# Gated attention and feed-forward on one core: scores and feed-forward in array tiles of 64 rows by 64 columns, P V in tiles of 64 by 32

## The chip, the core and the metric

The kernel runs on one core of a Trainium2 chip. The core has a matrix engine (TensorE, called PE in the profile, with its weight loads listed apart as PEld), a vector engine (VectorE, DVE), a scalar engine for activations (ScalarE, ACT), a general one (GpSimd, POOL), and a queue for transfers (SyncE, SP). The metric is the device time of one execution in microseconds (us); lower is better.

## What is computed

Two blocks read the same input `x` (2048 rows of 512) and are mixed row by row by a sigmoid gate. Block A is attention with 32 query heads of width 16 and one shared key and value head; block B is a feed-forward block with SiLU and 1792 hidden units. All arrays are float32.

```python
g = _sigmoid((x * gate_w).sum(-1, keepdims=True))
# A
q = (x @ wq).reshape(B, S, H, Dh).transpose(0, 2, 1, 3)      # H = 32, Dh = 16
k = x @ wk
v = x @ wv
p = _softmax(jnp.einsum("bhqd,bkd->bhqk", q, k) * Dh ** -0.5, axis=-1)
a = jnp.einsum("bhqk,bkd->bhqd", p, v)  # heads side by side, then @ wo
# B
b = _silu(x @ w1) @ w2
out = g * a + (1 - g) * b
```

## The kernel before

Matrix products that need float32 accuracy are made from float16 pieces: each operand is split into a float16 head and a float16 rest, and a product is the sum of three float16 products (head by head, head by rest, rest by head). A prologue transposes `x`, makes keys, values and the first queries, and splits the weights. Then `attention` runs, and nearly all of the time is spent there.

Attention goes in 32 rounds: 4 blocks of 512 query rows, 4 groups of 8 heads, and two halves of a group. A round has 16 steps, one for each 128 keys, and each step has two halves, so there are 1024 score slots in all. `scores` (L1348) makes one: two head pairs stand in the array's upper and lower 64 rows (50 of them used: the halves of q and k and the shift), and four matmuls with 32 keys each fill the 128 output rows, so 8 matmuls of 512 columns write one two-bank PSUM tile `S`. ScalarE then takes the exponent of the 128 by 1024 scores (L1369) into the float32 tile `P`. There are two `S` tiles, so the scores of half-step p wait for the exponent of half-step p-2.

`sums` (L1447) multiplies P by the values (called P V here, L1467). The stationary operand has 32 columns: the 16 value columns, a column of ones for the softmax sum, and digits. Four heads stand side by side in the 128 output rows, and the two head pairs' key halves use the upper and lower 64 rows: 8 matmuls in tiles of 64 by 32. A step is done either "native", in float32 (tile `VF`; all 512 columns in one go, or 256 and 256), or as an upper and a lower half-precision part (tiles `VP`, and `L`, which VectorE makes from P in a subtraction at L1388).

The feed-forward products, the output projection and the later query projections are a second stream of work on PE, dealt out in slots between the scores (`f_slot`, L1224). A slot holds one product of a new output block with its upper 64 rows of the contraction and one product of the block before it with its lower 64 rows: 4 + 4 matmuls of 512 columns through `Out.product` (L1007 to L1009). Where only one block is under way, the slot holds one half. ScalarE takes a tanh of each hidden block (L1023), VectorE and GpSimd finish it, and VectorE adds output blocks into accumulators (L983).

At the start of the attention loop the order of PE's work is a string written by hand, `FIRST`: S is a score slot and E one whole product of a query projection (`Out.whole`, L1013), which uses the array as one tile of 128 rows by 128 columns. After that, the order on PE, VectorE and GpSimd is fixed when the program is built, by a planner that keeps a clock for each engine: `SLOT` is its cost of a score or feed-forward slot, `VSLOT` and `NATIVE` those of P V, `issue(n, dur)` charges n instructions and dur us to PE's clock, and the `WAYS` table sets its preferences. Each engine executes its own instructions in that order and waits only on semaphores. When the last round ends, the remaining feed-forward blocks run as whole products.

Of the kernel before, what the change touches and what calls it, by code (L numbers as in the profile page):

```python
# [135 lines left out]
class Way:  # L136
# [7 lines left out]
    def set(self, p):  # L144
        for name, value in zip(self.names, WAYS[min(p // WAY_STEP, len(WAYS) - 1)]):
            setattr(self, name, value)
# [18 lines left out]
def kernel(  # L165
# [21 lines left out]
    nc = tc.nc  # L187
# [15 lines left out]
    KT = consts.tile([128, S], F16)  # L203
# [689 lines left out]
    def attention(ctx, scale_of, t_scale, shifts, split_pieces, chores, q_todo, bounds, early, gates_, later):  # L893
# [13 lines left out]
        def issue(n, dur):  # L907

            if sent[0] // 256 != (sent[0] + n) // 256:
                pe[0] = crossed[0] = max(pe[0], crossed[0] + BLOCK)  # L910
            sent[0] += n
            pe[0] += dur

        def put(dur, ready, due, f, hard=False, low=None, turns=False):

            tasks.append([due, ready, dur, f, hard, low, turns])
            return tasks[-1]
# [82 lines left out]
        class Out:  # L1000
# [5 lines left out]

            def product(self, n, rows, m, first, last):  # L1007
                l, r, i, j = self.mm[n]
                nc.tensor.matmul(self.bank[32 * m:32 * m + 32], l(i, rows, 32 * m), r(j, rows), start=first, stop=last)  # L1009

            def whole(self, n, first, last):
                l, r, i, j = self.mm[n]
# [148 lines left out]
        class Turn:  # L1161

            cur = new = None
            i = n = 0
# [47 lines left out]
        def leave(o):  # L1212

            t = o.evict(o.bank)
            f = t[3]

            def run():
                f()
                T_.free = dve[0] + 0.14

            t[3] = run
            T_.evicted = t

        def f_slot():  # L1224
            i, cur, new = T_.i, T_.cur, T_.new
            for m in range(4):
                if new and i < new.n:
                    new.product(i, lo, m, i == 0, False)
                if cur and i >= T_.n - cur.n:
                    cur.product(i - T_.n + cur.n, hi_, m, False, i == T_.n - 1)  # L1230
            issue(16, SLOT)
            if cur and i == T_.n - 1:
                leave(cur)
            T_.i += 1
            if T_.i == T_.n:
                T_.cur, T_.new, T_.going, T_.since, T_.chain = new, None, False, scored[0], bool(cur)
# [100 lines left out]
        def prefetch(i):  # L1337
            if i < len(rounds):
                c, o, rb = rounds[i]
                qtile[i] = qb_[i % 2]  # L1340
                if i:
                    assert not shifted or i == 1 or (o, c) in shifted
                    load_q(qtile[i], c, o, rb, shifts)

        probs, ends, low_end, lows, of_v, of_norm = {}, {}, {}, {}, [None], [None]
        qtile = {}

        def scores(p):  # L1348
            s, j = divmod(p, 2)
            i, kt = steps[s]  # L1350
            if p % 2 == 0 and kt == 0:
                prefetch(i + 1)
                if q_todo and i % 2 == 0:
                    queue.append(q_todo.pop(0))
            if j == 0:
                probs[s] = wp.tile([128, 4, 512], F32, name="P", bufs=PB)
            sc = pS.tile([128, 2, 512], F32, name="S")
            pe[0] = max(pe[0], ends.get(p - 2, 0.0) + 0.05)
            for m in range(4):
                for f in range(2):  # L1360
                    b = 64 * f
                    k0 = kt * 128 + 32 * m
                    nc.tensor.matmul(sc[32 * m:32 * m + 32, f], KT[b:b + 50, k0:k0 + 32], qtile[i][b:b + 50, j], start=True, stop=True)  # L1363
            issue(16, SLOT)
            begin = max(act[0], pe[0] + 0.48 - SLOT)
            scored[0] += 1
            P = probs[s]
            c, o, _ = rounds[i]
            nc.scalar.activation(P[:, 2 * j:2 * j + 2], sc, AF.Exp, scale=scale_of(c, o))  # L1369
            act[0] = begin + 0.904  # L1370
            ends[p] = begin + 1.018
            if j and s % 2 == 0:
                if s >= FIRST_LOW or not later:
                    lows[s] = put(LOW, ends[p] + 0.06, ends[p] + way.low2, lambda: low(s), low=lambda: len(L) < 2, turns=True)
                else:
                    native.add(s)
            elif j and s >= FIRST_LOW:
                lows[s] = put(LOW, ends[p] + 0.06, ends[p] + 40, lambda: low(s), low=lambda: len(L) < way.odd_l and s >= first[0] + way.spare, turns=True)
# [5 lines left out]
        def low(s):  # L1384

            P = probs[s]
            L[s] = wp.tile([128, 4, 512], F16, name="L", bufs=2)
            nc.vector.tensor_tensor(L[s], P, upper(P), op=OP.subtract)  # L1388
            low_end[s] = dve[0] + 0.06


        native, units, opened, first, v_end = set(), {}, set(), [0], [1e9 if later else 0.0]
# [101 lines left out]
        if early:  # L1494
            whole_ = early_products()
            for a in FIRST:
                if a == "S":
                    scores(p)
                    p += 1
                elif a == "E":  # L1500
                    next(whole_, None)
                elif bounds:
                    bound()
# [15 lines left out]
        while p < n_s:  # L1519
# [6 lines left out]
            if p % 2 == 0 and behind >= PB:  # L1526
                i = steps[s][0]
# [22 lines left out]
            if n is not None and first_sums:  # L1550
                sums(n, room)
            elif room >= SLOT and f_ready():
                f_slot()
            elif n is not None or sums_next(room) is not None and not (near and not fresh and last_unit(0) and behind < way.lastb):
                sums(n if n is not None else sums_next(room), room)
            else:
                k = next((k for k in waiting() if k % 2 == 0 and whole_step(k) and ends[2 * k + 1] + 0.05 <= pe[0]
                          and (not k // NKT or k // NKT in opened or closed_by(k // NKT - 1))), None)
                if k is not None and room >= 2 * SLOT:
                    make_native(k)  # L1560
                elif room >= SLOT and pe[0] + 0.02 < due:
                    pe[0] += 0.05
                else:
                    scores(p)
                    p += 1


        while first[0] < len(steps):
            serve(pe[0])
            n = sums_next(9.0)  # L1570
            if n is not None:
                sums(n)
            elif f_ready():
                f_slot()
            else:
                pe[0] += 0.05
        while T_.cur or T_.going:
            serve(pe[0])
            if not T_.going:
                nc.tensor.drain()  # L1580
                force(T_.evicted)
                T_.new, T_.i, T_.n, T_.going = None, 0, T_.cur.n, True
            f_slot()
# [60 lines left out]
```

## Time and profile before

| | us |
|---|---|
| median of the runs | 1034.26 |
| lowest and highest of 2 runs | 1033.28 and 1035.25 |
| the profiled execution's own time | 1035.51 |
| its span, first to last instruction | 1033.7 |
| mean granted TensorE clock in it | 0.998 |
| busy: PE, ACT, DVE, POOL | 1015.9, 992.8, 858.3, 388.3 |

Busy time on PE is the union of matmuls whose ends are modelled: matmuls overlap, and one of 512 columns is listed with about 375 ns although the next slot can start about 216 ns after it. So a PE that the profile calls busy may be waiting for up to some tenth of a us before each slot, and PE's work is better read from the starts of slots, in the view of instructions in order of time. There a row is the start, the length from the first start to the last end, the engine, the line, the operation with its tiles, the part of the array used (rows*columns), the operand's shape and type, and the count.

### The profile page before, as it was taken

How to read it: one execution, taken by the hardware profiler on the slowest of the kernel's cores; microseconds unless marked ns; L12 is line 12 of the kernel's file. 1: busy time of each engine (PE TensorE's matmuls, PEld its weight loads, DVE VectorE, ACT ScalarE, POOL GpSimd, SP SyncE). 2: the span in 40 equal slices, each digit the busy share in tenths (PEclk: the TensorE clock that was granted, in tenths of full speed). 3: DMA queues.
4: the chain of work that ended last, by engine and by line, in shares of the span. 5: the costliest groups of instructions: out<-in, count | busy, mean ns of one | idle time of the engine just before them, and what ended most of it. 6: DMA issues, size and time to landing. Idle time of an engine off the chain costs nothing.

```text
span 1033.7 us, 65235 instructions
## 1 busy us (share of the span) xinstructions
PE 1015.9 (98%) x30746; PEld 569.4 (55%) x30746; DVE 858.3 (83%) x867; ACT 992.8 (96%) x1116; POOL 388.3 (38%) x272
## 2 busy tenths in 40 slices
PE   7999999999999999999999999999999999999997
PEld 5455655555555556555555565555555565555553
DVE  6797988979899957787787887888897988888896
ACT  5899999999999999999999999999999999999990
POOL 2036116235032452524444315344352246383730
PEclk9999999999999999999999999999999999999999
DMA  7321211200000100000000010000000010000001
GB/s 257 90 63 52 65 54 43 63 12 23 12 15 31 32 22 12 12 21 6 22 23 12 22 53 10 17 12 12 23 12 12 9 47 13 12 12 12 5 4 45
DMA packets 23648, 32.92 MB, mean 32 GB/s; under 512 B 4985, under 2 KB 13338, under 8 KB 23370
## 3 DMA queue, kind: packets, MB, share of 16 engines
q1 hardware_dynamic: 22842, 28.49, 9.0%
q8 instruction: 242, 3.96, 1.7%
q14 instruction: 36, 0.29, 0.1%
q0 software_dynamic: 96, 0.10, 0.0%
q10 hardware_dynamic: 432, 0.07, 0.0%
HBM read 20.12 MB, written 8.52 MB: 28 GB/s over the span
## 4 chain that ended last, share of the span: by engine, by line
PE 52%; ACT 37%; issue 6%; DVE 5%; POOL 0%; ACTq 0%; DVEq 0%; POOLq 0%
ACT P L1369 35%; PE pm L1009 18%; PE pv L1467 17%; PE S L1363 13%; ACT e L1023 2%; DVE L L1388 2%; PE pt L449 1%; PE pm L1013 1%; PE pk L551 1%; PE S L1013 1%; DVE acc L983 0%; DVE T L1282 0%; DVE U L1283 0%; DVE w2s L320 0%; PE pq L244 0%
## 5 line engine op out<-in xcount | busy, mean ns | idle before, releaser
L1369 ACT ACTIVATE P<-S 128x1024 f32<-128x1024 f32 x1024 | 957.6, 1096 | 4.7 <-PE S L1363 2.5
L1388 DVE TENSOR_TENSOR L<-P 128x2048 f16<-128x2048 f32 x223 | 532.5, 2400 | 46.5 <-ACT P L1369 45.6
L1363 PE MATMUL S<-qb,KT 50*32 50x512 f16 x8192 | 441.0, 380 | 3.4 <-ACT P L1369 0.8
L1363 PEld LDWEIGHTS <-KT 50*32 50x32 f16 x8192 | 199.0, 89 | 254.3 <-issue 170.1
L1467 PE MATMUL pv<-P,VF 64*32 64x512 f32 (+1 forms) x5696 | 326.3, 511 | 0.0
L1009 PE MATMUL pm<-xs,w1s 64*32 64x512 f16 x5376 | 258.3, 375 | 0.6 <-DVE O L1251 0.6
L1009 PE MATMUL pm<-w2s,H 64*32 64x512 f16 x5088 | 252.2, 375 | 0.2 <-issue 0.2
L1288 POOL TENSOR_TENSOR T<-T,U 128x512 f32<-128x512 f32 x31 | 88.8, 2865 | 260.8 <-DVE U L1283 260.6
L1030 POOL CAST H<-e 128x512 f16<-128x512 f32 x56 | 67.0, 1197 | 251.3 <-DVE e L1028 246.2
L1009 PEld LDWEIGHTS <-w1s 64*32 64x32 f16 x5376 | 114.3, 92 | 47.3 <-issue 7.4
L1009 PEld LDWEIGHTS <-H 64*32 64x32 f16 x5088 | 111.7, 92 | 46.9 <-issue 5.4
L1467 PEld LDWEIGHTS pv<-P,VF 64*32 64x32 f32 x5696 | 114.8, 106 | 32.3 <-issue 4.3
L1031 POOL TENSOR_TENSOR H<-e,H 128x512 f16<-128x512 f32 x56 | 104.8, 1871 | 4.5
L1467 PE MATMUL pv<-P,VP 64*32 64x512 bf16 x1768 | 98.5, 387 | 0.0
L1467 PE MATMUL pv<-L,VP 64*32 64x512 f16 x1768 | 94.6, 374 | 0.2 <-DVE L L1388 0.2
L1009 PE MATMUL pm<-xs,wqs 64*32 64x512 f16 x1152 | 84.9, 375 | 0.1
L1467 PEld LDWEIGHTS <-VP 64*32 64x32 f16 x3536 | 60.8, 93 | 30.0 <-issue 8.5
L1028 DVE SCALAR_TENSOR_TENSOR e<-e,pm 128x512 f32<-128x512 f32 x56 | 38.4, 686 | 41.8 <-ACT e L1023 41.6
L1009 PE MATMUL pm<-wo_s,O 64*32 64x512 f16 x1440 | 66.5, 375 | 0.7 <-DVE acc L983 0.7
L1317 POOL CAST O<-T 128x512 f16<-128x512 f32 x15 | 21.1, 1409 | 67.1 <-DVE T L1315 56.3
L1290 POOL TENSOR_TENSOR T<-T 128x240 f32<-128x240 f32 x31 | 41.5, 1340 | 0.0
L983 DVE SCALAR_TENSOR_TENSOR acc<-pm,g,acc 128x512 f32<-128x512 f32 x43 | 32.1, 746 | 10.9 <-PE pm L1009 10.9
(176 smaller groups left out, 567.6 us busy)
## 6 DMA issues: line engine op xcount, KB each, us to landing
qb<-qd SPq DMA_DIRECT2D x189, 32.0 KB
raw<-in_B_w_dram SPq DMA_DIRECT2D x22, 256.0 KB
xn<-in_A_x_dram SPq DMA_DIRECT2D x8, 512.0 KB
out_dram<-acc SPq DMA_DIRECT2D x16, 256.0 KB
qd<-qx SPq DMA_DIRECT2D x12, 256.0 KB
w1r<-in_B_w_dram SPq DMA_DIRECT2D x2, 512.0 KB
raw<-in_A_wo_dram SPq DMA_DIRECT2D x4, 256.0 KB
qb<-sh SPq DMA_DIRECT2D x62, 2.0 KB
```

Source lines behind the costliest of these rows:

```text
L983: nc.vector.scalar_tensor_tensor(a, po, gate[:, n:n + 1], a, op0=OP.mult, op1=OP.add)
L1009: nc.tensor.matmul(self.bank[32 * m:32 * m + 32], l(i, rows, 32 * m), r(j, rows), start=first, stop=last)
L1028: nc.vector.scalar_tensor_tensor(e, e, 1.0, ph, op0=OP.add, op1=OP.mult)
L1030: nc.gpsimd.tensor_copy(H[:, 0], e)
L1031: nc.gpsimd.tensor_tensor(H[:, 1], e, H[:, 0], op=OP.subtract)
L1288: eng.tensor_tensor(T, T, U, op=OP.add)
L1290: eng.tensor_tensor(T3[:, :, 1:16], T3[:, :, 1:16], T3[:, :, 17:32], op=OP.add)
L1317: eng.tensor_copy(O[:, 0], OT)
L1363: nc.tensor.matmul(sc[32 * m:32 * m + 32, f], KT[b:b + 50, k0:k0 + 32], qtile[i][b:b + 50, j], start=True, stop=True)
L1369: nc.scalar.activation(P[:, 2 * j:2 * j + 2], sc, AF.Exp, scale=scale_of(c, o))
L1388: nc.vector.tensor_tensor(L[s], P, upper(P), op=OP.subtract)
L1467: nc.tensor.matmul(pvs[i][h][32 * j:32 * j + 32, cols], a[r], b[r, j, cols], start=start, stop=rest == n)
```

## The change

Scores and feed-forward slots use tiles of 64 rows by 64 columns: two matmuls with 64 stationary columns each take the place of four with 32, in each half of the array. The products and the bytes are the same. P V keeps its tiles of 64 by 32. The planner's costs and instruction counts (`issue(16, SLOT)`) are left as they were, so the order of slots on PE, and the order on ScalarE, VectorE, GpSimd and the transfer queue in the part of the program that runs, are the same as before. (A second pass behind a branch, for inputs outside certain ranges, is changed alike; it does not run.)

```diff
             def product(self, n, rows, m, first, last):
                 l, r, i, j = self.mm[n]
-                nc.tensor.matmul(self.bank[32 * m:32 * m + 32], l(i, rows, 32 * m), r(j, rows), start=first, stop=last)
+                nc.tensor.matmul(self.bank[64 * m:64 * m + 64], l(i, rows, 64 * m, 64), r(j, rows), start=first, stop=last)
...
         def f_slot():
             i, cur, new = T_.i, T_.cur, T_.new
-            for m in range(4):
+            for m in range(2):
                 if new and i < new.n:
                     new.product(i, lo, m, i == 0, False)
...
-            for m in range(4):
+            for m in range(2):
                 for f in range(2):
                     b = 64 * f
-                    k0 = kt * 128 + 32 * m
-                    nc.tensor.matmul(sc[32 * m:32 * m + 32, f], KT[b:b + 50, k0:k0 + 32], qtile[i][b:b + 50, j], start=True, stop=True)
+                    k0 = kt * 128 + 64 * m
+                    nc.tensor.matmul(sc[64 * m:64 * m + 64, f], KT[b:b + 50, k0:k0 + 64], qtile[i][b:b + 50, j], start=True, stop=True)
             issue(16, SLOT)
```

On PE, the end of a score slot and the beginning of the native P V step behind it, at the first such place of the program, before the change (the last two of 8 score matmuls; the numbers behind the names are buffer numbers; the shape is output rows x columns, so 32 or 64 stationary columns; a float32 matmul's weight load is part of it in this list):

```order
L1363 LDWEIGHTS KT_60
L1363 MATMUL S_648<-qb0_81,KT_60 32x512
L1363 LDWEIGHTS KT_60
L1363 MATMUL S_648<-qb0_81,KT_60 32x512
L1467 MATMUL pv0_658<-P_517,VF_62 32x512
L1467 MATMUL pv1_659<-P_517,VF_62 32x512
```

The same place with the change, where these are the last two of 4 score matmuls:

```order
L1363 LDWEIGHTS KT_60
L1363 MATMUL S_616<-qb0_81,KT_60 64x512
L1363 LDWEIGHTS KT_60
L1363 MATMUL S_616<-qb0_81,KT_60 64x512
L1467 MATMUL pv0_622<-P_517,VF_62 32x512
L1467 MATMUL pv1_623<-P_517,VF_62 32x512
```

Nothing stands in another place; the score slot has half as many instructions, and its tiles now have another width than those of the P V step behind it.

On PE again, where the lower half of a P V step in half precision is followed by a feed-forward slot (`w1s` and `xs` are the first layer's weights and the input), before:

```order
L1467 LDWEIGHTS VP_61
L1467 MATMUL pv1_1494<-L_2026,VP_61 32x512
L1009 LDWEIGHTS w1s_67
L1009 MATMUL pm_2039<-xs_66,w1s_67 32x512
L1009 LDWEIGHTS w1s_67
L1009 MATMUL pm_1852<-xs_66,w1s_67 32x512
```

And with the change:

```order
L1467 LDWEIGHTS VP_61
L1467 MATMUL pv1_1214<-L_1578,VP_61 32x512
L1009 LDWEIGHTS w1s_67
L1009 MATMUL pm_1587<-xs_66,w1s_67 64x512
L1009 LDWEIGHTS w1s_67
L1009 MATMUL pm_1472<-xs_66,w1s_67 64x512
```

Here too the order is the same, and the width of the tiles changes from 32 to 64 columns between the two lines. Counted over the part of the program that runs, PE's order has 27,889 matmuls before and 17,265 with the change (a float32 matmul is one here, and two in the trace). Consecutive matmuls pass 555 times from tiles of 64 by 32 to tiles of 64 by 64 and 554 times back; before, both kinds were 64 by 32.

## The prediction

> **What bounds the kernel now.** I read the engines' busy time first, then the chain of work that ended last, then PE's groups by shape.
>
> ```profile
> PE 1015.9 (98%) x30746; PEld 569.4 (55%) x30746; DVE 858.3 (83%) x867; ACT 992.8 (96%) x1116; POOL 388.3 (38%) x272
> PE 52%; ACT 37%; issue 6%; DVE 5%; POOL 0%; ACTq 0%; DVEq 0%; POOLq 0%
> L1363 PE MATMUL S<-qb,KT 50*32 50x512 f16 x8192 | 441.0, 380 | 3.4 <-ACT P L1369 0.8 <-DVE KT L571 0.5
> L1009 PE MATMUL pm<-xs,w1s 64*32 64x512 f16 x5376 | 258.3, 375 | 0.6 <-DVE O L1251 0.6
> L1009 PE MATMUL pm<-w2s,H 64*32 64x512 f16 x5088 | 252.2, 375 | 0.2 <-issue 0.2
> L1009 PE MATMUL pm<-xs,wqs 64*32 64x512 f16 x1152 | 84.9, 375 | 0.1
> L1009 PE MATMUL pm<-wo_s,O 64*32 64x512 f16 x1440 | 66.5, 375 | 0.7 <-DVE acc L983 0.7
> L1467 PE MATMUL pv<-P,VF 64*32 64x512 f32 x3616 | 243.2, 589 | 0.0
> L1467 PE MATMUL pv<-P,VF 64*32 64x256 f32 x2080 | 85.5, 376 | 0.0
> L1467 PE MATMUL pv<-P,VP 64*32 64x512 bf16 x1768 | 98.5, 387 | 0.0
> L1467 PE MATMUL pv<-L,VP 64*32 64x512 f16 x1768 | 94.6, 374 | 0.2 <-DVE L L1388 0.2
> L1369 ACT ACTIVATE P<-S 128x1024 f32<-128x1024 f32 x1024 | 957.6, 1096 | 4.7 <-PE S L1363 2.5
> ```
>
> PE and ACT are both close to full, and the last chain goes through both (52% and 37%). ACT's exponents alone (L1369) are 957.6 us. PE's 98% overstates its work, since modelled ends cover short waits; the starts of slots give it, in the instructions in order of time near the end of the loop:
>
> ```profile
> 1001.57 0.41 PE L1363 MATMUL S<-qb,KT 50*32 50x512 f16 x8
> 1001.79 1.05 PE L1467 MATMUL pv<-P,VF 64*32 64x512 f32 x16
> 1002.65 0.41 PE L1363 MATMUL S<-qb,KT 50*32 50x512 f16 x8
> 1002.87 0.84 PE L1009 MATMUL pm<-w2s,H 64*32 64x512 f16 x24
> 1003.51 0.41 PE L1363 MATMUL S<-qb,KT 50*32 50x512 f16 x8
> ...
> 1006.12 0.42 PE L1467 MATMUL pv<-P,VP 64*32 64x512 bf16 x8
> 1006.35 0.40 PE L1467 MATMUL pv<-L,VP 64*32 64x512 f16 x8
> 1006.56 0.41 PE L1363 MATMUL S<-qb,KT 50*32 50x512 f16 x8
> ```
>
> From 1002.65 to 1003.51 there is one score slot and three feed-forward slots (24 matmuls, 8 a slot): 0.86/4 = 0.215, so a slot costs 0.216 us within the rounding. A native P V step of 16 (float32 matmuls count twice) takes 1002.65 - 1001.79 = 0.86, one of 256 columns half of that, and a half-precision part (1006.56 - 1006.12)/2 = 0.22. The counts make the sum. Scores: 8192/8 = 1024 slots, 221 us. Feed-forward: 1,677 slots in the program's order (1,587 full and 90 with one half), 362 us. Native: 3616/16 x 0.86 = 194 and 2080/16 x 0.43 = 56. Halves: 3536/8 x 0.22 = 97. Together 930 us. The stretch they fill is
>
> ```profile
> 31.98 0.51 PE L1363 MATMUL S<-qb,KT 50*32 50x512 f16 x8 [0.46 <-DVE KT L571]
> ...
> 1013.21 2.12 PE L1009 MATMUL pm<-w2s,H 64*32 64x512 f16 x36 [0.16 <-issue]
> L1013 PE MATMUL pm<-xs,wqs 128*128 128x512 f16 x24 | 6.6, 382 | 0.0
> ```
>
> 981.2 us. In it stand also the 24 whole products of the last row (24 x 0.216 = 5 us) and their changes of shape (2 us), and some 2.6 us of feed-forward lies behind it, so PE's work is about 935 us and its waits are 46. Such a wait looks like this:
>
> ```profile
> 600.91 0.41 PE L1467 MATMUL pv<-L,VP 64*32 64x512 f16 x8
> 601.23 0.41 PE L1363 MATMUL S<-qb,KT 50*32 50x512 f16 x8
> 601.23 0.11 PEld L1363 LDWEIGHTS <-KT 50*32 50x32 f16 x7 [0.22 <-issue]
> ```
>
> The score slot starts 0.32 after a part that costs 0.22, and seven of its weight loads with it: it waited 0.10 for its S tile, which the exponent of two half-steps before still read, and no gap shows on PE since the matmuls before end late. The waits are mostly ACT's lead, then, and 46 us is all that a slower PE can hide behind.
>
> **What the change removes.** 4,096 score matmuls and 6,528 feed-forward matmuls go, with as many weight loads. A slot streams 512 columns either way, so I cost its length as unchanged. The trace has tiles of 64 columns in the prologue's keys, in pairs side by side:
>
> ```profile
> 18.41 0.64 PE L449 MATMUL pt<-ident,xn 128*128 128x128 f32 x4
> 18.98 0.84 PE L551 MATMUL pk<-xs,wkvs 128*64 128x512 f16 x6
> 19.74 0.75 PE L449 MATMUL pt<-ident,xn 128*128 128x128 f32 x4
> 20.42 4.72 PE L551 MATMUL pk<-xs,wkvs 128*64 128x512 f16 x42
> L551 PEld LDWEIGHTS <-wkvs 128*64 128x64 f16 x48 | 2.5, 110 | 2.3
> ```
>
> 42 matmuls in 21 pairs take 4.72, of which the last pair's length is 0.38: 4.34/20 = 0.217 a pair. So two tiles run at once, weights of 64 columns (110 ns a load, against 89 to 92 for 32) load beside them, and a slot of two tiles is as long as one of eight. Two row halves at once are what every slot of before has. Four tiles of 64 by 64 together stand nowhere in the trace; from the pair I take no change of the slot, with 0.01 us more as the near upper end; both a gain and a larger loss are rivals below.
>
> The Trainium skill ("TensorE: Matmul & The Clock Gate", Measured speedup vs the span model) has a pack of tiles last one matmul plus about 4 ns for each further tile; four tiles fewer would be 16 ns a slot, over the 2,701 slots of scores and feed-forward an estimated 43 us less, a sum of 1,085 with the price below. The pair's row speaks against counting that, since the next slot begins before the span of the one before has ended.
>
> **What it adds.** Before, scores, feed-forward and P V all use 64 by 32. With the change, PE's order passes 1,109 times between 64 by 32 and 64 by 64. No such pair of shapes is in the trace, but the array does change shape at the loop's start, between score slots and whole products:
>
> ```profile
> 32.96 0.41 PE L1363 MATMUL S<-qb,KT 50*32 50x512 f16 x8
> 33.30 0.82 PE L1013 MATMUL pm<-xs,wqs 128*128 128x512 f16 x3
> 34.05 0.41 PE L1363 MATMUL S<-qb,KT 50*32 50x512 f16 x8
> 34.39 0.82 PE L1013 MATMUL pm<-xs,wqs 128*128 128x512 f16 x3
> ...
> 37.33 0.41 PE L1363 MATMUL S<-qb,KT 50*32 50x512 f16 x8
> ```
>
> A score slot and three whole products repeat four times from 32.96 to 37.33, so every 4.37/4 = 1.09 us, where the same four slots without a change of shape take 0.86: 0.23 for two changes, 0.115 each. Singly: 34.39 - 34.05 - 0.216 = 0.124 leaving 64 by 32, and 34.05 - 33.30 - 0.648 = 0.102 entering it. Waiting data are no reason here, as the period is the same each time. The keys' rows show a change of columns alone, 128 rows staying: 19.74 - 18.98 - 3 x 0.216 = 0.112. That is the nearest row to a change from 64 to 32 columns, and it agrees. I take 0.114, with 0.102 and 0.124 as the near ends, and 0 and 0.16 as the far ones: below nothing a change can't go, and 0.16 is a whole matmul's tail, its 0.38 less the 0.216 of a slot. The sum: 1,109 x 0.114 = 126 us on PE.
>
> The Trainium skill ("TensorEngine Tiling (Array Packing)", Key Properties) says that changing the tiling mode, and not only the tile, drains TensorE; it gives no price, and the rows agree that every change costs. Its page "TensorE: Matmul & The Clock Gate" (Step-by-step) puts the drain at about 128 cycles, 53 ns at 2.4 GHz, by which the changes would be an estimated 59 us and the sum below 1,061.
>
> **The sum.** Order on the other engines is unchanged, so they wait for PE. PE's work in the loop becomes 935 + 126 = 1061, ACT's exponents stay at 957.6, and ACT gets behind PE only where a few short slots follow one another. So I let 32 of the 46 us of waits go, and keep 14 for the loop's starts, tile evictions and such places. Span: 1033.7 + 126 - 32 = 1127.7. The profiled execution's own time lies 1.8 above its span (1035.51), which makes 1129.5, and it is 1.25 above the median 1034.26: 1128 us.
>
> **Rivals.**
> 1. *The change of shape is free where the rows stay at 64* (the other side: not slower). The array would keep both widths at once and just pick columns. For it: no row shows this pair, and scores, feed-forward and P V do mix freely now. Against: 0.112 where only columns changed. It decides where a change costs less than 46/1,109 = 0.04 us, which the waits would cover: 1034. That half as many instructions would bring it below, nothing shows: PE's idle time put down to issue is 0.2 us. Chance 0.06.
> 2. *Half the price.* With half the rows of the whole products, half the price: 0.057 x 1,109 = 63, so 1034 + 63 - 32 = 1065. For it: the rows of the price have whole products on one side. (The Trainium skill's drain, cited above, is of this size.) Against: 0.124 was paid leaving 64-row tiles and 0.102 leaving 128-row ones, so fewer rows aren't cheaper. Chance 0.07, taken from 1050 to 1090.
> 3. *Slots shorten with fewer tiles.* Eight starts spread a slot to 0.41 from 0.38 for one matmul; if slots followed one another by such spans, 2,701 x 0.02 = 54 us would go, with free changes 980, with my price 1074. (It is what the Trainium skill's span rule, cited above, would mean here.) Against: 0.217 for pairs and 0.216 for eight. Chance 0.02, half of it faster.
> 4. *Slots lengthen.* If a 64-column load is not covered when four tiles run, or two of the four take turns, the slots grow: 0.04 x 2,701 = 108 and 1236 for the first, a whole 0.216 more each, 583 us and 1711, for the second. Against: the pairs, and the row halves running at once. Chance 0.06.
>
> **How the numbers follow.** My own case has 0.79. Its low end is 1,109 x 0.102 = 113 with all 46 hidden: 1034 + 67 = 1101, and I reach down to 1090 for a part of rival 2; its high end is 1,109 x 0.124 = 138, only 18 hidden, and 0.01 on 2,701 slots (27): 1034 + 147 = 1181. So 1090 to 1180. About 2% is what a measurement tells from no change here (1014 to 1055): rival 1 lies within it, 0.05, but for 0.01 on the fast side; with rival 3's half that makes faster 0.02, same 0.05, slower 0.93.
>
> **What would show it.** Right: in the instructions in order of time, a score slot followed by P V starts it 0.32 to 0.34 later instead of 0.216, and a P V part in front of a score slot likewise, while score to feed-forward stays at 0.216; ACT's busy share falls to about 992.8/1128 = 88%, with idle time before L1369 ended by PE's S. Wrong: score-to-P V starts at 0.22 (rival 1) or 0.27 (rival 2), feed-forward slots back to back below 0.20 (rival 3) or above 0.23 (rival 4), or ACT still at 95% with a longer span, which would mean that something other than PE holds it.

## The result and the profile after

The changed kernel takes 1142.38 us (1142.25 to 1142.52 in two runs) against 1034.26: a ratio of 1.1048, 95% interval 1.103 to 1.1066, so slower by 108 us. The forecast was 1128, between 1090 and 1180. The profiled execution took 1142.25 with a span of 1140.4, at a granted clock of 0.998 as before.

From its page, the busy time of each engine, the chain that ended last (by engine and by line), and the groups that answer to those shown of before:

```profile
PE 1127.7 (99%) x20122; PEld 429.6 (38%) x20122; DVE 858.8 (75%) x867; ACT 1028.5 (90%) x1116; POOL 358.1 (31%) x272
...
PE 98%; DMA 1%; ACT 0%; DVE 0%; SPq 0%; issue 0%; ACTq 0%
PE pv L1467 37%; PE pm L1009 33%; PE S L1363 25%; PE S L1013 1%; PE pm L1013 1%; PE pt L449 1%; DMA xn<-in_A_x_dram 1%; PE pk L551 0%; PE pm L511 0%; ACT P L1369 0%; PE pq L244 0%; PE pq L246 0%; PE pq L245 0%; DVE KT L571 0%; PE pv L578 0%
...
L1369 ACT ACTIVATE P<-S 128x1024 f32<-128x1024 f32 x1024 | 988.2, 1029 | 76.6 <-PE S L1363 64.0
...
L1363 PE MATMUL S<-qb,KT 50*64 50x512 f16 x4096 | 414.0, 388 | 0.5 <-DVE KT L571 0.5
```

A third of PE's instructions are gone (20,122 matmuls, 30,746 before), and PE is busier. The chain that was shared between PE (52%) and ACT (37%) is now PE's alone, 98%. ACT, which stood idle 4.7 us before its exponents, now waits 76.6 us, 64.0 of them for PE's scores.

Where PE's time goes is read from the starts of slots. In order of time, with the start, the length to the last end, the line, the tiles, the part of the array and the count:

```profile
600.66 0.41 PE L1363 MATMUL S<-qb,KT 50*64 50x512 f16 x4
601.00 1.09 PE L1467 MATMUL pv<-P,VF 64*32 64x512 f32 x16
602.01 0.41 PE L1363 MATMUL S<-qb,KT 50*64 50x512 f16 x4
602.25 0.38 PE L1009 MATMUL pm<-wo_s,O 64*64 64x512 f16 x1
...
604.64 0.39 PE L1363 MATMUL S<-qb,KT 50*64 50x512 f16 x4
604.96 0.42 PE L1467 MATMUL pv<-P,VP 64*32 64x512 bf16 x8
605.20 0.40 PE L1467 MATMUL pv<-L,VP 64*32 64x512 f16 x8
605.52 0.40 PE L1009 MATMUL pm<-wo_s,O 64*64 64x512 f16 x1
...
1007.70 0.39 PE L1363 MATMUL S<-qb,KT 50*64 50x512 f16 x4
1007.92 0.82 PE L1009 MATMUL pm<-xs,w1s 64*64 64x512 f16 x12
1008.57 0.39 PE L1363 MATMUL S<-qb,KT 50*64 50x512 f16 x4
```

Where the shape stays, nothing has changed: a score slot and three feed-forward slots take 1008.57 - 1007.70 = 0.87 for four, 0.217 each. Where it changes, a score slot before P V takes 604.96 - 604.64 = 0.32 in place of 0.216, or 601.00 - 600.66 = 0.34 if it stands behind P V too, and the half-precision part before feed-forward 605.52 - 605.20 = 0.32 in place of 0.22. The slot right behind a change is also a little longer: 602.25 - 602.01 = 0.24 for a score slot with no change after it, and the native step 602.01 - 601.00 = 1.01 pays both, 0.86 before.

I added this up over every slot of the loop in both traces: the start of the next slot less its own start, less 0.216 (a half-precision part 0.219, eight records of a float32 product of 512 columns 0.430). Before, the slots at the 17 changes seen take 2.2 us beyond their length and all others 41.5, which are the waits. After, the slots at 1,123 changes take 138.8 and all others 15.6, most of it the longer slot behind a change and not a wait. So the slots at the changes cost 136.6, 0.123 each, and 25.9 us went away elsewhere, net 110.7. The loop, from its first score slot to its last P V, grew by 108.5 (31.98 to 1012.64 before, 30.56 to 1119.67 after). Missing records are not the reason for the 2 us between, as the counts of the two traces differ by just the 10,624 matmuls that the change removes; in the trace of before some slots start in two parts, which makes grouping them uncertain.

The longer slot behind a change belongs to the price, too. With it the changes cost about 150 us, 0.135 each, and of the 41.5 us of waits only some 2 are left. By kind, with the two halves of a native step taken singly, the medians are: 0.101 out of a wide slot, or 0.124 where that slot stands behind a change itself; 0.108 to 0.143 from a half-precision part into a wide slot, and 0.136 from a native step; and 0.022 on average for a slot that only stands behind a change.

The weight loads show what goes with the later start:

```profile
604.64 0.39 PE L1363 MATMUL S<-qb,KT 50*64 50x512 f16 x4
604.96 0.14 PEld L1467 LDWEIGHTS <-VP 64*32 64x32 f16 x16 [0.32 <-issue]
604.96 0.42 PE L1467 MATMUL pv<-P,VP 64*32 64x512 bf16 x8
...
605.55 0.12 PEld L1363 LDWEIGHTS <-KT 50*64 50x64 f16 x4
605.76 0.39 PE L1363 MATMUL S<-qb,KT 50*64 50x512 f16 x4
```

Where the shape stays, a slot's loads start with the slot before it, 0.21 ahead (605.55 and 605.76). Behind a change the first load starts together with the first matmul (604.96 both), at 705 of the 706 score and half-precision slots of this trace that stand there.

### The profile page after: what moved, and what is told of

It is laid out like the page before. It is cut to its first block, busy times and chain, and to the rows that moved or that the text cites. A ratio compares the mean times of both kernels' runs of the same rounds, so it can differ in the third digit from the quotient of the medians.

```text
span 1140.4 us, 43987 instructions
## 1 busy us (share of the span) xinstructions
PE 1127.7 (99%) x20122; PEld 429.6 (38%) x20122; DVE 858.8 (75%) x867; ACT 1028.5 (90%) x1116; POOL 358.1 (31%) x272
## 4 chain that ended last, share of the span: by engine, by line
PE 98%; DMA 1%; ACT 0%; DVE 0%; SPq 0%; issue 0%; ACTq 0%
PE pv L1467 37%; PE pm L1009 33%; PE S L1363 25%; PE S L1013 1%; PE pm L1013 1%; PE pt L449 1%; DMA xn<-in_A_x_dram 1%; PE pk L551 0%; PE pm L511 0%; ACT P L1369 0%; PE pq L244 0%; PE pq L246 0%; PE pq L245 0%; DVE KT L571 0%; PE pv L578 0%
## 5 line engine op out<-in xcount | busy, mean ns | idle before, releaser
L1369 ACT ACTIVATE P<-S 128x1024 f32<-128x1024 f32 x1024 | 988.2, 1029 | 76.6 <-PE S L1363 64.0
L1363 PE MATMUL S<-qb,KT 50*64 50x512 f16 x4096 | 414.0, 388 | 0.5 <-DVE KT L571 0.5
L1363 PEld LDWEIGHTS <-KT 50*64 50x64 f16 x4096 | 129.8, 104 | 321.0 <-issue 270.2
L1009 PE MATMUL pm<-xs,w1s 64*64 64x512 f16 x2688 | 248.2, 376 | 0.0
L1009 PE MATMUL pm<-w2s,H 64*64 64x512 f16 x2544 | 241.9, 377 | 0.2 <-issue 0.2
L1009 PEld LDWEIGHTS <-w1s 64*64 64x64 f16 x2688 | 99.5, 106 | 75.0 <-issue 18.9
L1009 PEld LDWEIGHTS <-H 64*64 64x64 f16 x2544 | 96.6, 106 | 69.1 <-issue 15.1
L1467 PEld LDWEIGHTS pv<-P,VF 64*32 64x32 f32 x5696 | 71.3, 105 | 95.8 <-issue 84.7
L1467 PE MATMUL pv<-P,VP 64*32 64x512 bf16 x1768 | 92.8, 395 | 0.0
L1009 PE MATMUL pm<-xs,wqs 64*64 64x512 f16 x576 | 82.1, 377 | 0.0
L1009 PE MATMUL pm<-wo_s,O 64*64 64x512 f16 x720 | 64.5, 377 | 0.0
```

Of the source, the lines that this page charges most:

```text
L1009: nc.tensor.matmul(self.bank[64 * m:64 * m + 64], l(i, rows, 64 * m, 64), r(j, rows), start=first, stop=last)
L1363: nc.tensor.matmul(sc[64 * m:64 * m + 64, f], KT[b:b + 50, k0:k0 + 64], qtile[i][b:b + 50, j], start=True, stop=True)
L1467: nc.tensor.matmul(pvs[i][h][32 * j:32 * j + 32, cols], a[r], b[r, j, cols], start=start, stop=rest == n)
```

## The experiments

The times go with runs of the kernel before on the same chip, whose medians were 1033.48 us (first four), 1034.42 (the next three) and 1033.55 (the last two). The number of changes of shape is counted in each program's order.

**Only the scores wide.** Feed-forward back to the old loop, so that a score slot stands alone between narrow ones:

```diff
-            for m in range(4):
+            for m in range(2):
                 for f in range(2):
...
-                    k0 = kt * 128 + 32 * m
-                    nc.tensor.matmul(sc[32 * m:32 * m + 32, f], KT[b:b + 50, k0:k0 + 32], qtile[i][b:b + 50, j], start=True, stop=True)
+                    k0 = kt * 128 + 64 * m
+                    nc.tensor.matmul(sc[64 * m:64 * m + 64, f], KT[b:b + 50, k0:k0 + 64], qtile[i][b:b + 50, j], start=True, stop=True)
```

> Only the score slots use 64 by 64; feed-forward stays at 64 by 32 like P V. So fewer matmuls are wide than in the change (4,096 of 10,624), but a score slot now stands between narrow ones nearly everywhere: 2,022 changes of shape instead of 1,109. Theory (each change costs about 0.124 us on a PE that has some 40 us of waits to hide it in): 2,022 x 0.124 = 251, less about 38 hidden, so 1247 us. Rival (the 64-column tiles themselves are slow, and the changes cost nothing): 39% of the loss of 108 us, so about 1076.

Measured: 1250.89 us. With fewer wide matmuls than the change it is slower than the change by 108.5, as the count of changes says and the count of wide matmuls doesn't. Its order of time shows each score slot paying on both sides:

```profile
1220.06 0.41 PE L1363 MATMUL S<-qb,KT 50*64 50x512 f16 x4
1220.39 0.63 PE L1009 MATMUL pm<-w2s,H 64*32 64x512 f16 x16
1220.84 0.41 PE L1467 MATMUL pv<-P,VP 64*32 64x512 bf16 x8
1221.07 0.40 PE L1467 MATMUL pv<-L,VP 64*32 64x512 f16 x8
1221.39 0.41 PE L1363 MATMUL S<-qb,KT 50*64 50x512 f16 x4
```

Scores to feed-forward is 0.33 here, where the change had 0.22; feed-forward to P V, both narrow now, is 0.45 for two slots.

**Only feed-forward wide.** The other half of the change:

```diff
-                nc.tensor.matmul(self.bank[32 * m:32 * m + 32], l(i, rows, 32 * m), r(j, rows), start=first, stop=last)
+                nc.tensor.matmul(self.bank[64 * m:64 * m + 64], l(i, rows, 64 * m, 64), r(j, rows), start=first, stop=last)
...
-            for m in range(4):
+            for m in range(2):
                 if new and i < new.n:
```

> Only the feed-forward slots use 64 by 64; scores stay at 64 by 32 like P V: 1,291 changes of shape. Theory: 1,291 x 0.124 = 160, less about 30 hidden: 1164 us, slower than the whole change. Rival (slow wide tiles): 61% of the loss of 108 us, so about 1100.

Measured: 1158.17. Either half alone is worse than both together, since scores and feed-forward often follow one another and then share a shape.

**Everything wide.** The change, and P V in 64 by 64 as well, so that hardly a change is left. The kernel leaves out the P V of two heads of four; its P V slots stream as many columns as before:

```diff
-                a, b, cols, n = VP[:, k], upper(P) if u[0] == "U" else L.pop(s), slice(0, 512), 1
+                a, b, cols, n = VP[:, min(k, NKT - 2):min(k, NKT - 2) + 2].rearrange("p a b -> p (a b)"), upper(P) if u[0] == "U" else L.pop(s), slice(0, 512), 1
...
-            for j in range(4):
+            for j in range(2):
                 for h, r in enumerate((lo, hi_)):
-                    nc.tensor.matmul(pvs[i][h][32 * j:32 * j + 32, cols], a[r], b[r, j, cols], start=start, stop=rest == n)
+                    nc.tensor.matmul(pvs[i][h][64 * j:64 * j + 64, cols], a[r], b[r, j, cols], start=start, stop=rest == n)
```

> Everything in the loop uses 64 by 64, P V too: it computes two of the four heads of each step with 64 stationary columns in 4 matmuls, so its slot streams as many columns as before and the other two heads' P V is left out. 29 changes of shape remain in the loop. Theory: nothing but those is paid, 1034 + 4, less what is hidden: 1030 to 1038 us. Rival (slow wide tiles): at least the 1142 of the change, since there are more wide tiles now. Rival (a slot shortens with fewer tiles): below 1010.

Measured: 1034.09, 1.0002 times the kernel before (0.9991 to 1.0013). Wide tiles cost nothing, and they bring nothing either, although half of PE's instructions are gone. Engines, chain and exponents on its page are again those of before:

```profile
PE 1014.9 (98%) x15506; PEld 602.4 (58%) x15506; DVE 856.7 (83%) x867; ACT 992.7 (96%) x1116; POOL 387.4 (38%) x272
...
PE 53%; ACT 35%; issue 5%; DVE 4%; DMA 1%; POOL 0%; ACTq 0%; DVEq 0%
...
L1369 ACT ACTIVATE P<-S 128x1024 f32<-128x1024 f32 x1024 | 958.4, 1109 | 4.9 <-PE S L1363 3.1
```

**More work, no change of shape.** The kernel before, with every second score slot done twice:

```diff
+            for again in range(1 + p % 2):
                 for m in range(4):
                     for f in range(2):
...
```

> The kernel before, all in 64 by 32, with every second score slot done twice (the second run writes the same numbers): 512 x 0.216 = 111 us more work on PE, no change of shape. Theory (PE is full, so that any work on it beyond some 26 to 41 us of waits lengthens the kernel): 1034 + 111 - 30 = 1115 us, within 10. Rival (PE has much more room, and what the change costs comes from its effect on other engines): below 1080.

Measured: 1113.75, so 80 of 111 us show and 31 are hidden. Work on PE lengthens the kernel without any change of shape, beyond what the waits hide, and the chain turns to PE:

```profile
PE 97%; DVE 1%; ACT 1%; POOL 0%; issue 0%; POOLq 0%; DVEq 0%; ACTq 0%
```

**The planner told of the price.** The change, with

```diff
-        def issue(n, dur):
+        def issue(n, dur, cols=64):
+            if scored[0] > 100 and shape[0] not in (None, cols):
+                pe[0] += 0.114
+            shape[0] = cols
...
-            issue(16 if u[0] in "UL" else 32, VSLOT if u[0] in "UL" else n * NATIVE)
+            issue(16 if u[0] in "UL" else 32, VSLOT if u[0] in "UL" else n * NATIVE, 32)
```

> The change, with the planner told of the price: from the 100th score slot on, its PE clock pays 0.114 us at each change of shape, so that the order on all engines is planned on a true clock. The new order has 1,183 changes of shape (74 more, +9 us at 0.124) and about 9 us less of other PE work (fewer native P V steps, and 360 products moved behind the loop as whole ones). Theory (PE is the bound and runs without waits, so a better plan has nothing to recover): 1142 us, within 10. Rival (much of the loss comes from an order planned for another clock): below 1110.

Measured: 1161.80, a miss by 10 us on the slow side. The same sum over its slots gives 152.1 at the changes (138.8 in the change) and 34.1 elsewhere (15.6): 13 + 18 us more, while the kernel grew by 19. The remaining 12 are put down to less plain work, of which 9 were expected. I had left out that the new order loses time elsewhere, spread over the whole loop, which I did not follow further. The rival, that much of the loss came from an order planned for another clock, would have given less than 1110. This order does not bear it out, and with some 2 us of waits left in the change another order could win little but by fewer changes.

**One tile of 128 columns.** The change, with scores and feed-forward in tiles of 64 rows by 128 columns, two matmuls a slot:

```diff
...
-            for m in range(2):
+            for m in range(1):
                 for f in range(2):
                     b = 64 * f
-                    k0 = kt * 128 + 64 * m
+                    k0 = kt * 128
-                    nc.tensor.matmul(sc[64 * m:64 * m + 64, f], KT[b:b + 50, k0:k0 + 64], qtile[i][b:b + 50, j], start=True, stop=True)
+                    nc.tensor.matmul(sc[128 * m:128 * m + 128, f], KT[b:b + 50, k0:k0 + 128], qtile[i][b:b + 50, j], start=True, stop=True)
```

> Scores and feed-forward in tiles of 64 rows by 128 columns, two matmuls a slot, P V unchanged: 1,110 changes of shape between 128 and 32 columns, at the places of the change. Theory (a change costs the same whichever widths it passes between): 1142 us, within 12. Rival (the price comes from loading the wider weights behind the change): twice the columns, so about 0.02 to 0.05 more at half of the changes, 1155 to 1170; or slots of two tiles no longer fit in 0.216, which would add at least 27.

Measured: 1133.13, 9 us less than the change at the same places of change. Wider weights do not cost more; the change out of a slot is a little cheaper:

```profile
601.72 0.38 PE L1363 MATMUL S<-qb,KT 50*128 50x512 f16 x2
602.03 1.09 PE L1467 MATMUL pv<-P,VF 64*32 64x512 f32 x16
603.05 0.39 PE L1363 MATMUL S<-qb,KT 50*128 50x512 f16 x2
603.37 0.42 PE L1467 MATMUL pv<-P,VP 64*32 64x512 bf16 x8
```

The two score slots take 0.31 and 0.32 before P V, where the change has 0.32 and 0.34. Summed over its slots, the changes take 131.0 in place of 138.8, or 0.116 each by the reckoning that gave 0.123.

**Fewer changes by bursts of P V.** The change, with a price of 0.12 a change on the planner's clock, and its choice from the 300th half-step on replaced by

```diff
+                k = next((k for k in waiting() if can_go(k)), None)
+                if shape[0] == 64:
+                    burst[0] = 0
+                if k is not None and (burst[0] or behind >= 4) and burst[0] < 6:
+                    burst[0] += len(units_of(k))
+                    while units_of(k) and can_go(k):
+                        sums(k)
+                elif room >= SLOT and f_ready():
+                    f_slot()
+                else:
+                    scores(p)
+                    p += 1
```

> The change, with the order planned so that P V comes in bursts of up to three steps (it waits until four steps are scored) from the 300th half-step on: 753 changes of shape instead of 1,109, and about 6 us less of other PE work. Theory: 356 x 0.124 = 44 and 6 less than the change where no new waits come, 1092; bursts leave ACT without scores at times and PE then waits for it, up to 20 more: 1092 to 1112 us. Rival (the loss doesn't go by the number of changes): 1136 or more.

Measured: 1205.40, a miss by over 90 us and within the range of the rival (1136 or more). The changes did get fewer and their sum smaller, 109.2 at 767 in place of 138.8 at 1,123. But the slots elsewhere take 116.4 beyond their length, 15.6 in the change. The order of time shows what they are, behind a burst of P V, and the waits view sums them up (engine, line, what ended the wait: us, times, longest):

```profile
558.54 0.42 PE L1472 MATMUL pv<-P,VP 64*32 64x512 bf16 x8
558.77 0.40 PE L1472 MATMUL pv<-L,VP 64*32 64x512 f16 x8
558.99 1.04 PE L1472 MATMUL pv<-P,VF 64*32 64x512 f32 x16
559.96 0.63 PE L1368 MATMUL S<-qb,KT 50*64 50x512 f16 x8
560.42 0.60 PE L1014 MATMUL pm<-xs,w1s 64*64 64x512 f16 x8
561.50 0.41 PE L1368 MATMUL S<-qb,KT 50*64 50x512 f16 x4 [0.48 <-ACT P L1374]
562.41 0.41 PE L1368 MATMUL S<-qb,KT 50*64 50x512 f16 x4 [0.50 <-ACT P L1374]
...
ACT P L1374 <- PE S L1368: 122.3, 175, 2.9
...
PE S L1368 <- ACT P L1374: 71.1, 162, 1.0
```

A burst outlasts the two score tiles, so ACT runs dry and waits for PE (122.3 us); then PE does scores back to back and waits for ACT's exponents (71.1). The burst traded changes for a wait on each side. Part of the loss is PE's clock, too: its mean was 0.99, and in the third of these stretches of 20, 10 and 20 us it is full again (the columns are the stretch, its length, busy time of each engine, the clock, the DMA share and GB/s).

```profile
680.00:700.00 20.00, 17.24 (x278) 6.31 (x270) 15.14 (x13) 17.98 (x20) 8.56 (x5) 0.95 0.09 25
700.00:710.00 10.00, 9.45 (x132) 3.04 (x125) 5.75 (x8) 5.76 (x8) 4.44 (x3) 0.76 0.08 28
710.00:730.00 20.00, 19.23 (x352) 7.99 (x351) 13.82 (x9) 16.90 (x18) 0.00 (x0) 1.00 0.13 46
```

So this run says nothing against the price, and nothing for it beyond its smaller sum. To count changes without another order, I took two doses in the kernel before.

**Doses: every fourth and every second score slot wide.** The kernel before, with w = 64 where `p % 4 == 1` (or `p % 2 == 1`) and 32 elsewhere:

```diff
-            for m in range(4):
+            w = 64 if p % 4 == 1 else 32
+            for m in range(128 // w):
...
-                    nc.tensor.matmul(sc[32 * m:32 * m + 32, f], KT[b:b + 50, k0:k0 + 32], qtile[i][b:b + 50, j], start=True, stop=True)
+                    nc.tensor.matmul(sc[w * m:w * m + w, f], KT[b:b + 50, k0:k0 + w], qtile[i][b:b + 50, j], start=True, stop=True)
```

> The kernel before, in its own order, with every fourth score slot alone in 64 by 64: 508 changes of shape, 1,024 wide matmuls. Theory (0.13 us a change, counting what the slot behind it loses, with 26 to 41 us of waits to hide it in): 508 x 0.13 = 66, less 15 to 35: 1065 to 1085 us. Rival (by wide matmuls): a tenth of 108 us, 1045. Rival (single changes are all hidden, and only many are paid): 1034 to 1045.

> The same with every second score slot in 64 by 64: 1,016 changes of shape, 2,048 wide matmuls. Theory: 1,016 x 0.13 = 132, less 20 to 35: 1131 to 1146 us, so twice as many changes cost the full 0.13 each beyond the first 508 (63 to 69 us more). Rival (by wide matmuls): a fifth of 108 us, 1055.

Measured: 1068.29 for every fourth (1.0338 times before, 1.0321 to 1.0355), and 1126.35 for every second, 5 under its expectation. The second dose cost 58 us where 63 to 69 were expected. The rivals are out: by wide matmuls it would have been 1045 and 1055, and with single changes hidden at most 1045. Each time over the kernel before of its own call, by the number of changes of shape, with the time that a further change adds:

| kernel | changes | us more than before | us for each change beyond the row above |
|---|---|---|---|
| everything wide | 29 | 0.6 | |
| every fourth score slot | 508 | 34.7 | 0.071 |
| every second score slot | 1,016 | 92.8 | 0.114 |
| the change | 1,109 | 108.1 | 0.165 |
| only feed-forward wide | 1,291 | 124.7 | 0.091 |
| only scores wide | 2,022 | 217.4 | 0.127 |

From 508 to 2,022 it is (217.4 - 34.7)/1,514 = 0.121 each, and the line meets zero at 34.7/0.121 = 287 fewer than 508, at 221 changes. By this line the first 221 or so, 27 us, would disappear in waits. The traces divide it otherwise. Summed over the slots, with the slot behind a change counted to the price, the changes cost 68, 132, 149, 162 and 260 us in the five kernels below the first row, 0.126 to 0.135 each; what the kernels grew by is less by 34 to 43 us, the waits that went. So the steep and the flat step in the middle (0.165 and 0.091) are mostly the price itself: it rises by 17 us over 93 changes, and by 13 over 182, since the kernels differ in the kinds of change.

The chain with every fourth slot shows the cover nearly used up (ACT 6%, 37% before):

```profile
PE 89%; ACT 6%; DVE 3%; issue 1%; POOL 0%; ACTq 0%; DVEq 0%; POOLq 0%
```

## Why the prediction was right

- *PE and ACT both near full, 46 us of waits on PE.* Right. Summed over all slots it was 41.5. The prediction let 32 of them go. Doubling score slots hid 31 us, but the change hid more, some 39, and left 2.
- *Slots unchanged by wide tiles.* Right: 0.217 in the change, and 1.0002 times before with everything wide. Rivals 3 and 4, shorter or longer slots, fall with that run. By the span rule of the Trainium skill ("TensorE: Matmul & The Clock Gate", Measured speedup vs the span model) four tiles fewer make a pack an estimated 16 ns shorter. The traces agree on the span, which went from 0.41 for a score slot to 0.39 where the shape stays; but the next pack starts inside it, 0.217 after the start, and nothing is gained.
- *Each change costs about 0.114.* The mechanism was right, the term was too small: 136.6 us in place of 126 at the changes themselves, 0.123 each, and about 150 with the longer slots behind them, 0.135 each. The price read from the loop's start was the mean of one period with whole products, where one slot in four stood behind a change alone, and was 0.010 longer. Here 752 slots do, 0.022 longer each, 17 us in all. The 554 changes out of wide slots cost 63 us, as forecast; the 555 from P V into them cost 70, as those out of a native step are dearer (0.136). Rival 1 (free where the rows stay at 64) and rival 2 (half the price) are out: only columns change here, and it costs as much as any change in the trace of before. The Trainium skill ("TensorEngine Tiling (Array Packing)", Key Properties) has it that changing the tiling mode drains TensorE; every run agrees that a change costs, and none shows the drain itself. The estimate of 59 us from the drain of about 128 cycles in the Trainium skill ("TensorE: Matmul & The Clock Gate", Step-by-step) was less than half of what the 1,109 changes cost.
- *The sum.* +126 - 32 = +94 was forecast; by the traces it was about +150 - 39 = +111 in the loop, and +108 was measured. So the price was 24 us too small and the cover 7 us too small, and that the two errors partly cancel is luck. The order left as it was is not shown to be to blame: planned with the price it was slower still (1161.80).
- *What would show it.* Score slot to P V 0.32 to 0.34, and scores to feed-forward 0.216 with the shape kept, as forecast. ACT's share fell to 90%, not 88%, since its exponents overlap less when each waits for PE and their union grew from 957.6 to 988.2.

What is not settled is how the price splits, between waiting for the array to be empty and loading weights that were not loaded ahead. The trace shows that the loads start late together with the matmuls, and such a load lasts 89 to 106 ns on average, about as long as the slot before it is lengthened. So the two can't be told apart here.

## What to carry to other kernels

Count how often consecutive matmuls pass from one tile shape to another before widening a tile in one part of an interleaved stream; here it is 0.12 to 0.135 us each time, more than half a slot of 512 columns, even when only the columns change. Fewer and wider tiles don't shorten a slot that already fills its rate with small ones, so there was nothing on the other side. If shapes must differ, group the work by shape, but only as far as the buffers between the engines carry it: a burst longer than two score tiles cost more in waits than it saved in changes. No run here shows a grouping that gains.

## What the runs showed that I had not expected

Half the instructions gave nothing at all: with everything wide 15,506 matmuls and as many loads took 1034.09 where 30,746 had taken 1033.48, in as many slots of the same length. The slot right behind a change is 0.24 long in place of 0.216. Tiles of 128 columns, the widest, changed shape most cheaply (0.116 against 0.123). Weights are loaded a slot ahead where the shape stays, and not across a change. And in the burst kernel, with ACT and PE waiting for each other, the granted clock fell to 0.76 over 10 us; what brought it down is not shown.
